# The down projection's weights: one transfer of 1.75 MiB in place of two halves

## The chip, the cores and the metric

The kernel runs on one core of a Trainium2 chip. The metric is the device time of one execution in microseconds. Three runs of the kernel before took 213.03, 213.16 and 212.81 us, a median of 213.03 us.

A core has five engines that run on their own and meet only through semaphores: TensorE (PE in the profile, with its weight loads listed as PEld), VectorE (DVE), ScalarE (ACT), GpSimd (POOL) and SyncE (SP). In this kernel SP issues nearly all the DMA transfers, one after the other in the order of its program.

## What is computed

The input is `x` of 2048 rows by 512 columns, in bf16. It is layer-normalised, and two blocks read the result. The output is the sum of three terms.

```python
xn = _layernorm(x)
# block A, linear attention with 32 heads of 16
qkv = xn @ wqkv                        # 512 -> 3 * 512, split into q, k, v
phi = lambda t: where(t > 0, t + 1, exp(t)) + 1e-6
kv  = einsum("bhsd,bhse->bhde", phi(k), v)
z   = einsum("bhsd->bhd", phi(k))
o   = (phi(q) @ kv) / (phi(q) . z + 1e-6)
A   = o @ wo                           # 512 -> 512
# block B, a gated feed-forward net with F = 1792
B   = (silu(xn @ w_gate) * (xn @ w_up)) @ w_down
out = x + A + B
```

The weights this document is about are those of the last product: `w_down`, 1792 rows by 512 columns in bf16, which is 1.75 MiB.

## The kernel before, in words

The 2048 rows are cut into 16 tiles of 128 rows, and four tiles make a chunk of 512 columns of the transposed input. F is cut into 14 blocks of 128.

First part. Each tile is loaded, normalised and transposed into `xnT`. TensorE projects it to k and q (L421), ScalarE, GpSimd and VectorE apply phi, and TensorE gathers the sum over rows of normalised input times phi(k) in four PSUM banks (L470). The order of all these steps is written out by hand, as a string of words that `run` reads (from L562 on). A letter names the step and a number the tile, so `Q11` is the q projection of tile 11. The letter `T` takes one of the big weight loads from the list `BIG` (L548). `T0` is the first half of the gate weights, `T5` and `T4` the second halves of the up and gate weights, and `T6` and `T7` the two halves of the down weights. `U0` and `U1`, near the end of the string, are the first two gate and up blocks.

Second part. A loop over 56 steps `j` (four chunks of 14 blocks) multiplies the gate and the up weights with `xnT` (`gu`, L524). ScalarE applies silu to the gate product (L532) and VectorE multiplies it with the up product into `hT` (L537). Between these steps lie the rest of the attention (the products at L582 and L648, the sum `z` turned by a DMA at L598 and spread over partitions by the transfers at L605 and L607, the division, and the transposes by DMA at L641). The output tiles come in the chunks after the first: `otile` runs when the block number is 5, 8, 11 or 13, and tiles 12 to 15 follow the loop, the last of them in three cuts. An output tile is one PSUM accumulation of 4 products with the attention part (L654) and 14 products with the down weights (L658). VectorE adds `x` (L664) and SP stores the tile (L667).

How order and waits come about. Every step calls `K.add` with an engine, its instructions, the keys it reads and the keys it writes. `number` works out from the keys which earlier operations each one waits for, and leaves out a wait that the engine is known to have passed. `emit` then writes each engine's program in the order of the calls. So the order of the words matters only among steps of one engine. A transfer has a semaphore of its own. Every load goes through the helper at L184 and is known in the profile by its tile.

The down weights are kept whole in `wd`, 14 blocks of 512 columns on each partition. `dload` (L205) loads seven blocks. Its two calls are the last two entries of `BIG`, both on SP and with nothing of SP's between them: the words between `T6` and `T7` give work to the other engines only. Both loads write a key of their own, nobody has read or written `wd` before, and so neither waits for anything. The only reader is the second half of `ogroup` at L658, which names both keys. The first output tile is therefore the first that waits for them.

Of the kernel before, what the change touches and what calls it, by code (L numbers as in the profile page):

```python
# [10 lines left out]
P = 128  # L11
# [7 lines left out]
NFC = F // P  # L19
# [92 lines left out]
def bass_parallel_sum__linear_attn_block__swiglu_ffn__prompt_kernel(nc, A_x, A_wqkv, A_wo, B_x, B_w_gate, B_w_up, B_w_down, out):  # L112
    xin = A_x[0]
    oview = out[0]
    K = _Program()
    bf, f32 = dt.bfloat16, dt.float32

    with contextlib.ExitStack() as es:
        E = es.enter_context

        def sb(name, shape, dtype):
            return E(nc.sbuf_tensor(name, shape, dtype))
# [15 lines left out]
        wd = sb("wd", [P, NFC, D], bf)  # L138
        pk = sb("pk", [P, NT, D], bf)
        pq = sb("pq", [P, NT, D], bf)  # L140
        hT = sb("hT", [P, 2, NFC, 512], bf)
# [37 lines left out]
        def B(i):  # L179
            return ("bank", i)  # L180


        def load(eng, key, dst, src):
            K.add(eng, lambda e: e.dma_start(dst, src), w=[key], dma=True)  # L184
# [14 lines left out]
        def fload(eng, key, dst, src, h):  # L199
            load(eng, (key, h), dst[:, :, h * FH:(h + 1) * FH],  # L200
                 src[:, h * FH:(h + 1) * FH].rearrange("(c p) f -> p c f", p=P))

        WD_LO = (0, 7)

        def dload(eng, lo):  # L205
            load(eng, ("wd", lo), wd[:, lo:lo + 7, :],
                 B_w_down[lo * P:(lo + 7) * P, :].rearrange("(c p) f -> p c f", p=P))


        K.add("act", lambda e: e.preload_act_table_set("natural_log_exp_and_others"))  # L210
# [332 lines left out]
        def pair(j):  # L543
# [4 lines left out]
        BIG = [lambda: fload("sp", "wg", wg, B_w_gate, 0), lambda: fload("sp", "wu", wu, B_w_up, 0),  # L548
               lambda: wload("sp", 2), lambda: woload("sp"),
               lambda: fload("sp", "wg", wg, B_w_gate, 1), lambda: fload("sp", "wu", wu, B_w_up, 1),  # L550
               lambda: dload("sp", WD_LO[0]), lambda: dload("sp", WD_LO[1])]
        steps.update({"U": pair, "T": lambda t: BIG[t]()})

        def run(text):
# [14 lines left out]
            T2 K14 u9 P0 s10 x14 K7 n10 S12 R11 u10 m14 x7 m7 T3 Q6 S8 y6 R12 G10 K6 s14 R8 P12 D12 n6 x6 Q7 s7  # L569
            S15 L8 R15 G7 m6 u6 y7 s6 Q14 y14 D8 G14 Q12 P11 K12 n7 u7 y12 Q8 L15 x12 n14 n12 D0 m12 u14 D11 K8  # L570
            u12 s12 y8 n8 G6 G12 x8 K11 u8 m8 D15 s8 Q11 x11 K15 T0 Q15 y11 G8 x15 m11 T5 s11 y15 n11 m15 G11 T4
            u11 T6 n15 s15 u15 U0 G15 U1 T7
        """)

        def gt_evac(c, eng):
# [76 lines left out]
        def ogroup(bank, t, lo, hi):  # L652
            C, jj = t // 4, t % 4
            fns = [(lambda e, g=g: e.matmul(  # L654
                banks[bank][:, 0:hi - lo], pk[:, t, g * P:(g + 1) * P], M[:, g, lo:hi],
                start=(g == 0), stop=False)) for g in range(NG)]
            K.add("pe", fns, r=[("pk", t)] + [("M", g) for g in range(NG)], w=[B(bank)])
            fns = [(lambda e, fc=fc: e.matmul(  # L658
                banks[bank][:, 0:hi - lo], hT[:, C % 2, fc, jj * P:(jj + 1) * P], wd[:, fc, lo:hi],
                start=False, stop=(fc == NFC - 1))) for fc in range(NFC)]  # L660
            K.add("pe", fns, r=[("hT", C % 2, fc) for fc in range(NFC)] + [("wd", lo_) for lo_ in WD_LO], w=[B(bank)])

        def oout(bank, t, lo, hi):
            K.add("dve", lambda e: e.tensor_tensor(  # L664
# [5 lines left out]
        def otile(t):  # L670
            b = t % 4
            ogroup(b, t, 0, D)
            oout(b, t, 0, D)
# [8 lines left out]
        for j in range(NGU):  # L682
            C, fc = j // NFC, j % NFC
# [33 lines left out]
        for b, lo, hi in cuts:  # L717
            ogroup(b, 15, lo, hi)
            oout(b, 15, lo, hi)
# [37 lines left out]
```

## Time and profile before

| | |
|---|---|
| median of three runs | 213.03 us (212.81 to 213.16) |
| the profiled execution | 213.13 us, of which the span of its instructions is 211.9 us |
| clock granted to TensorE | 1.00 |
| busy: PE, DVE, ACT, POOL | 207.1, 124.5, 68.4, 67.1 us |
| read from HBM, written to it | 9.96 MB, 2.10 MB |

The span runs from the first to the last instruction of the program. A view called the chain of waits goes back from the last instruction, at each step to what released it. A group is all instructions of one line, engine, operation and tile, with the mean duration of one. Matmuls are pipelined, so their durations overlap, and the distance from one start to the next is shorter than the duration of one. Idle time of an engine stands with what ended it. For a transfer the profile gives the time that its issue took on the queue of the issuing engine, and the time from issue to landing. "SPq" is SP's queue. A view in windows gives the busy time of each engine in a stretch, the clock granted to TensorE, the mean busy share of the 16 DMA engines and the rate at which they moved bytes.

### The profile page before, as it was taken

The numbers are of one execution on the slowest core, as the hardware profiler recorded it, in microseconds if no ns is written. First come the engines' busy times: TensorE is split into PE (matmuls) and PEld (weight loads), VectorE is DVE, ScalarE is ACT, GpSimd is POOL, SyncE is SP. The second block draws the span as 40 slices with busy tenths as digits, with TensorE's granted clock in tenths as the row PEclk, the third lists the DMA queues.
The fourth block names the chain that finished last, engine by engine and source line by source line (L and its number), as shares of the span: only waits on it lengthen the run. The fifth ranks groups of instructions, "written<-read, shape, count | busy, mean of one in ns | idle before, by whom it ended". The sixth has DMA issues, their size and how long they took to land.

```text
span 211.9 us, 2730 instructions
## 1 busy us (share of the span) xinstructions
PE 207.1 (98%) x994; PEld 97.1 (46%) x1013; DVE 124.5 (59%) x223; ACT 68.4 (32%) x146; POOL 67.1 (32%) x95
## 2 busy tenths in 40 slices
PE   7999999999999999999999999999999999999995
PEld 3534444444544444444444444444444444444455
DVE  3799998653996368454644773464457473535121
ACT  5994656554344333031221322130123031220000
POOL 3795688649950162202202121202202220000000
DMA  5963547599501201120101110111010111011001
GB/s 164 359 197 77 124 102 223 101 338 365 164 0 25 53 0 25 24 53 25 25 25 46 28 29 25 25 50 25 28 33 20 23 50 50 3 50 47 27 28 51
DMA packets 28750, 16.44 MB, mean 78 GB/s; under 512 B 18624, under 2 KB 28608, under 8 KB 28736
## 3 DMA queue, kind: packets, MB, share of 16 engines
q1 hardware_dynamic: 27872, 15.48, 26.3%
q10 hardware_dynamic: 864, 0.79, 1.1%
q8 instruction: 8, 0.13, 0.3%
q14 instruction: 6, 0.05, 0.1%
HBM read 9.96 MB, written 2.10 MB: 57 GB/s over the span
## 4 chain that ended last, share of the span: by engine, by line
PE 93%; ACT 3%; DMA 1%; issue 1%; DVE 1%; POOL 0%
PE pb L524 45%; PE pb L658 23%; PE pb L421 11%; PE pb L654 7%; PE pb L470 6%; ACT ef L439 1%; DMA x_sb<-in_A_x_dram 1%; PE pb L382 0%; PE pb L582 0%; PE pb L648 0%; DVE stats L254 0%; ACT rstd L263 0%; ACT lnv L261 0%; ACT xnT L356 0%; PE pb L244 0%
## 5 line engine op out<-in xcount | busy, mean ns | idle before, releaser
L532 ACT ACTIVATE sil<-pb 128x512 bf16<-128x512 f32 x56 | 33.4, 597 | 104.1 <-PE pb L524 102.5
L537 DVE TENSOR_TENSOR hT<-pb,sil 128x512 bf16<-128x512 f32 x56 | 38.2, 682 | 38.1 <-PE pb L524 37.5
L524 PE MATMUL pb<-xnT,wg 128*128 128x512 bf16 x224 | 57.8, 379 | 0.0
L524 PE MATMUL pb<-xnT,wu 128*128 128x512 bf16 x214 | 55.8, 379 | 0.5
L658 PE MATMUL pb<-wd,hT 128*128 128x512 bf16 (+2 forms) x247 | 51.1, 355 | 0.3
L615 POOL TENSOR_TENSOR pz<-pq,zbc 128x512 f32<-128x512 bf16 x16 | 22.3, 1395 | 91.4 <-DVE den L622 79.1
L658 PEld LDWEIGHTS pb<-wd,hT 128*128 128x128 bf16 x252 | 23.6, 98 | 24.9
L524 PEld LDWEIGHTS pb<-xnT,wu 128*128 128x128 bf16 x224 | 21.9, 98 | 26.0
L524 PEld LDWEIGHTS pb<-xnT,wg 128*128 128x128 bf16 x224 | 21.9, 98 | 25.9
L664 DVE TENSOR_TENSOR out_sb<-pb,x_sb 128x512 bf16<-128x512 f32 (+2 forms) x18 | 11.4, 632 | 35.8 <-PE pb L658 35.8
L421 PE MATMUL pb<-wqkv,xnT 128*128 128x512 bf16 x102 | 23.8, 379 | 0.5 <-ACT xnT L356 0.4
L442 ACT ACTIVATE ef<-pb 128x512 bf16<-128x512 f32 x26 | 15.3, 593 | 12.5 <-PE pb L421 12.5
L449 POOL TENSOR_SCALAR ef<-ef 128x512 bf16<-128x512 bf16 x26 | 15.9, 615 | 8.7 <-ACT ef L442 8.7
L654 PE MATMUL pb<-M,pk 128*128 128x512 bf16 (+2 forms) x72 | 16.8, 355 | 0.0
L421 PEld LDWEIGHTS pb<-wqkv,xnT 128*128 128x128 bf16 x104 | 10.1, 98 | 12.9 <-ACT xnT L356 0.9
L254 DVE BATCH_NORM_STATS2 stats<-x_sb 128x6 f32<-128x512 bf16 x16 | 10.8, 678 | 3.5 <-DMA x_sb<-in_A_x_dram 3.5
L470 PE MATMUL pb<-pk,xn 128*128 128x512 bf16 x51 | 12.8, 379 | 0.1
L637 DVE TENSOR_TENSOR pq<-pq,rden 128x512 bf16<-128x512 bf16 x16 | 12.6, 786 | 0.0
L622 DVE TENSOR_REDUCE den<-pz 128x32 f32<-128x512 f32 x16 | 10.8, 676 | 0.0
L493 POOL TENSOR_TENSOR zacc<-zacc,pk 128x512 f32<-128x512 f32 x8 | 10.2, 1278 | 0.6
L460 DVE SCALAR_TENSOR_TENSOR pk<-pb,ef 128x512 bf16<-128x512 f32 x13 | 8.7, 679 | 2.6 <-POOL ef L449 2.6
L460 DVE SCALAR_TENSOR_TENSOR pq<-pb,ef 128x512 bf16<-128x512 f32 x13 | 8.8, 682 | 2.5 <-POOL ef L449 2.4
(70 smaller groups left out, 112.6 us busy)
## 6 DMA issues: line engine op xcount, KB each, us to landing
x_sb<-in_A_x_dram SPq DMA_DIRECT2D x15, 128.0 KB, 4.6
out_dram<-out_sb SPq DMA_DIRECT2D x15, 128.0 KB, 1.7
wu<-in_B_w_up_dram SPq DMA_DIRECT2D x2, 896.0 KB, 7.1
wg<-in_B_w_gate_dram SPq DMA_DIRECT2D x2, 896.0 KB, 7.1
wd<-in_B_w_down_dram SPq DMA_DIRECT2D x2, 896.0 KB, 12.9
wqkv<-in_A_wqkv_dram ACTq DMA_DIRECT2D x5, 128.0 KB, 4.8
wqkv<-in_A_wqkv_dram SPq DMA_DIRECT2D x1, 512.0 KB, 4.1
wo<-in_A_wo_dram SPq DMA_DIRECT2D x1, 512.0 KB, 4.9
```

What stands on the lines that cost most here:

```text
L421: fns.append(lambda e, c=c, first=first, last=last: e.matmul(banks[b][:, :], src[:, c, t * P:(t + 1) * P], wqkv[:, c, col:col + D], start= ...
L442: K.add("act", lambda e: e.activation(buf, banks[b][:, :], ACT.Exp), r=[B(b)], w=[bkey])
L449: K.add("pool", lambda e: e.tensor_scalar(out=buf, in0=buf, scalar1=top, scalar2=0.0, op0=ALU.min, op1=ALU.max), r=[bkey] + tkeys, w=[bkey])
L460: K.add("dve", lambda e: e.scalar_tensor_tensor(out=dst, in0=val, scalar=low, in1=mid, op0=ALU.max, op1=ALU.add), r=keys + lkeys, w=[dkey])
L470: K.add("pe", [(lambda e, c=c: e.matmul(banks[c][:, :], src[:, t, c * P:(c + 1) * P], pk[:, t, :], start=first, stop=last)) for c in range ...
L524: fns.append(lambda e, c=c, b=b, w_=w_: e.matmul(banks[b][:, :], w_[:, c, fc * P:(fc + 1) * P], xnT[:, c, C * 512:(C + 1) * 512], start=(c ...
L532: K.add("act", lambda e: e.activation(sil[:, j % 2, :], banks[gb(j)][:, :], ACT.Silu), r=[B(gb(j))], w=[("sil", j % 2)])
L537: K.add("dve", lambda e: e.tensor_tensor(out=hT[:, C % 2, fc, :], in0=banks[gb(j) + 1][:, :], in1=sil[:, j % 2, :], op=ALU.mult), r=[B(gb( ...
L615: K.add("pool", lambda e: e.tensor_tensor(out=pz[:, t % 2, :].rearrange("q (g p) -> q g p", g=NG), in0=pq[:, t, :].rearrange("q (g p) -> q ...
L637: K.add("dve", lambda e: e.tensor_tensor(out=heads(pq[:, t, :]), in0=heads(pq[:, t, :]), in1=rden[:, i, :][:, :, None].broadcast_to([P, NH ...
L654: fns = [(lambda e, g=g: e.matmul(banks[bank][:, 0:hi - lo], pk[:, t, g * P:(g + 1) * P], M[:, g, lo:hi], start=(g == 0), stop=False)) for ...
L658: fns = [(lambda e, fc=fc: e.matmul(banks[bank][:, 0:hi - lo], hT[:, C % 2, fc, jj * P:(jj + 1) * P], wd[:, fc, lo:hi], start=False, stop= ...
```

## The change

The two loads of seven blocks become one load of fourteen. `BIG` loses an entry, the string loses its last word `T7`, and the reader at L658 names one key instead of two. The transfer's place in SP's order is that of `T6`.

```diff
-        WD_LO = (0, 7)
-
-        def dload(eng, lo):
-            load(eng, ("wd", lo), wd[:, lo:lo + 7, :],
-                 B_w_down[lo * P:(lo + 7) * P, :].rearrange("(c p) f -> p c f", p=P))
+        def dload(eng):
+            load(eng, ("wd",), wd[:, :, :], B_w_down.rearrange("(c p) f -> p c f", p=P))
...
-               lambda: dload("sp", WD_LO[0]), lambda: dload("sp", WD_LO[1])]
+               lambda: dload("sp")]
...
-            u11 T6 n15 s15 u15 U0 G15 U1 T7
+            u11 T6 n15 s15 u15 U0 G15 U1
...
-            K.add("pe", fns, r=[("hT", C % 2, fc) for fc in range(NFC)] + [("wd", lo_) for lo_ in WD_LO], w=[B(bank)])
+            K.add("pe", fns, r=[("hT", C % 2, fc) for fc in range(NFC)] + [("wd",)], w=[B(bank)])
```

## The prediction

> **What bounds the kernel now.** I read the page first, then the chain of waits in order of time, then what PE waited for, and last the down weights themselves: when they are issued, when they land, and when they are first used.
>
> The page, its head, its slices and its shares of the chain:
>
> ```profile
> span 211.9 us, 2730 instructions
> PE 207.1 (98%) x994; PEld 97.1 (46%) x1013; DVE 124.5 (59%) x223; ACT 68.4 (32%) x146; POOL 67.1 (32%) x95
> ...
> PE   7999999999999999999999999999999999999995
> ...
> DMA  5963547599501201120101110111010111011001
> ...
> PE 93%; ACT 3%; DMA 1%; issue 1%; DVE 1%; POOL 0%
> ```
>
> TensorE is busy in every slice but the first and the last, and 93% of the chain that ended last is its work. The DMA engines are full in slices 8 to 10 only; a slice is 211.9 / 40 = 5.3 us, so that is about 42 to 58 us. That is where the down weights travel.
>
> The chain of waits in order of time (start, duration, what), some of its pieces, and all that PE waited for over the whole span (total, times, longest):
>
> ```profile
> 0.81 2.65 DMA x_sb<-in_A_x_dram
> ...
> 12.52 1.90 PE pb L421 x8
> ...
> 46.36 1.73 PE pb L470 x8
> ...
> 165.53 3.02 PE pb L658 x14
> ...
> 209.69 0.29 DVE out_sb L664
> ```
>
> ```profile
> PE pb L244 <- PEq L742: 0.8, 1, 0.8
> PE pb L421 <- ACT xnT L356: 0.4, 1, 0.4
> PE pb L382 <- POOL nmb L368: 0.3, 1, 0.3
> ```
>
> PE waits three times, 1.5 us together. The last of the waits is the one that ends at 12.52 us, where the chain passes from ACT to PE for good. From there to the last product of the output the chain stays on PE, to 209.69 us, and the only other pieces are issue gaps of 0.05 us. So 197 of 211.9 us are one unbroken row of matmuls. A change helps only by having fewer of them, closer together, or by a shorter head (12.5 us) or tail (2.2 us). It hurts only by opening a hole in the row.
>
> **The change part by part.** First, when the weights come and when they are wanted. The instructions that touch the tile `wd` (duration in ns, min/median/max, first and last start in us; the time to landing below), then the same restricted to the first of the two loads:
>
> ```profile
> L658 PEld LDWEIGHTS pb<-wd,hT x252: 97/98/98, 85.7 to 209.4; 128*128 128x128 bf16 x126
> ...
> L184 SPq DMA_DIRECT2D wd<-in_B_w_down_dram x2: 793/1950/3108, 42.8 to 43.6; - x2
> ...
> DMA to landing us min/median/max: 12.1/12.9/13.7
> ```
>
> ```profile
> L184 SPq DMA_DIRECT2D wd<-in_B_w_down_dram x1: 793/793/793, 42.8 to 42.8; - x1
> ...
> DMA to landing us min/median/max: 12.1/12.1/12.1
> ```
>
> The first half is issued at 42.8 us and lands 12.1 us later, at 54.9. The second is issued at 43.6 and lands 13.7 us later, at 57.3. The first instruction that reads `wd` is a weight load at 85.7 us. The slack is 85.7 - 57.3 = 28.4 us.
>
> *The landing of the single transfer.* The bytes are the same, 2 x 896 KB, and they stand behind the same gate and up weights. The stretches around them (PE busy, PEld, DVE, ACT, POOL, clock, DMA share, GB/s):
>
> ```profile
> 46.00:48.00 2.00, 2.00 (x11) 0.94 (x10) 1.66 (x3) 1.72 (x3) 1.53 (x3) 1.00 1.05 392
> ...
> 54.00:55.00 1.00, 1.00 (x5) 0.46 (x5) 1.00 (x2) 0.00 (x0) 0.92 (x2) 1.00 1.10 348
> 55.00:56.00 1.00, 0.95 (x6) 0.48 (x6) 1.00 (x2) 0.60 (x1) 0.92 (x2) 1.00 0.44 138
> 56.00:57.00 1.00, 1.00 (x12) 0.65 (x11) 1.00 (x2) 0.00 (x0) 0.92 (x2) 1.00 0.06 20
> 57.00:58.00 1.00, 1.00 (x13) 0.65 (x11) 1.00 (x3) 0.60 (x1) 1.00 (x1) 1.00 0.00 0
> ```
>
> The engines are full up to 55 us and empty from 57. The pipe has no hole that merging could close, so the last byte cannot come much before 56. I take 57 us. The bounds: 55 us, where the full stretch ends, and 70.2 us, if the one transfer took as long as both in turn (42.8 + 2 x 13.7). Even the late end leaves 15.5 us before 85.7. Cost on the path: 0. If the cover were gone, each microsecond of landing after 85.7 would be a microsecond of the kernel.
>
> Here a rule can be held against the rows. The two halves land 57.3 - 54.9 = 2.4 us apart, and 917,504 bytes at 348 GB/s take 2.6 us, so the second pays nothing beside its bytes. The Trainium skill, "DMA: Bandwidth & Descriptors", section "Anatomy of one DMA", fits each transfer of another issuing path with about 2.0 us fixed plus its bytes. By that fixed cost, paid in turn, the merged transfer would land some 2 us sooner, an estimate from the page; the trace does not agree for transfers queued behind each other, and the sum is the same either way.
>
> *The halves' separate keys.* A half that lands early could let an early reader start. The only reader names both keys, and both are down 28.4 us before it. Cost 0.
>
> *SP's queue.* The issues in time (start, duration):
>
> ```profile
> 41.06 0.58 SPq L184 DMA_DIRECT2D wg<-in_B_w_gate_dram  x1
> ...
> 42.79 3.94 SPq L184 DMA_DIRECT2D wd<-in_B_w_down_dram  x2
> 64.21 1.20 SPq L598 DMA_TRANSPOSE zT<-zb  x1
> 67.67 0.34 SPq L605 DMA_DIRECT2D zrow<-zc  x1
> ```
>
> The two issues hold SP to 46.7 us, the second longer (3.1 us) than the first (0.8 us), as if it had to wait for room. One issue is removed. What the longer one costs the trace does not show: at least 0.34 us, as the shortest issue in these rows, at most twice 3.94 = 7.9 us. I take 3.9, since the same number of pieces must fit. SP is then free between 43.1 and 50.7 us. What is next on SP is the transpose of `z` at 64.21, which is not late for SP's sake: `z` is summed only in step 6 of the loop. At least 13.5 us of cover. Cost 0, gain 0. No transfer is moved past another: `T0`, `T5` and `T4` stay ahead.
>
> *The gate weights, which are tight.* The tile `wg` within 40 to 70 us:
>
> ```profile
> L524 PEld LDWEIGHTS pb<-xnT,wg x48: 97/98/98, 47.7 to 70.0; 128*128 128x128 bf16 x48
> ...
> L184 SPq DMA_DIRECT2D wg<-in_B_w_gate_dram x2: 507/544/580, 41.1 to 42.2; - x2
> ...
> DMA to landing us min/median/max: 5.3/7.1/8.9
> ```
>
> The first half of `wg` is issued at 41.06 and lands 5.3 us later, at 46.4; PE reads it at 47.7. The margin is only 1.3 us, the smallest that I found near the edit. But this load is issued 1.7 us before the down weights, in the same queue, so its bytes stand ahead of theirs before and after. Bounds: a gain of 0, since PE does not wait there, and a loss of 0 unless it landed 1.3 us later. I take 0.
>
> *TensorE's program.* The first L658 group loses one of its two waits for `wd`. There is no hole in PE's row there, so a wait passed long ago costs nothing that shows. Bounds: the 0.05 us of an issue gap, and 0. I take 0.
>
> *Contention between transfers and matmuls.* The 8 matmuls from 46.36 us, under 392 GB/s, take 1.73 us, 0.216 each; the 14 from 165.53, with little traffic, take 3.02, also 0.216. The full pipe does not slow PE now, and one transfer cannot fill it fuller. Cost 0.
>
> The sum: 213.13 us, the profiled execution's own time (span 211.9, the other 1.2 us around it), plus 0. It stands 0.1 us above the median of 213.03, so I predict 213.0 us.
>
> **The rivals.**
>
> *Slower: fewer DMA engines carry the merged transfer.* A transfer of another shape could be spread over fewer of the 16. The down bytes begin to flow when the second half of `wg` is down, at 42.2 + 8.9 = 51.1 us, and PE needs them at 85.7. 1,835,008 bytes in 34.6 us are 53 GB/s; an engine carries 348 / 16 = 21.75 GB/s, so it decides from two engines downward. With two: 42.2 us, landing at 93.3, 7.6 us of stall, 220.6 us. Against it: the halves, of the same layout, keep all 16 engines at a share of 1.10. The Trainium skill, "DMA: Bandwidth & Descriptors", section "Why a DMA increments its semaphore by 16 and not by 1", says that the slowest dimension of both patterns decides the number of engines. If that were the 14 blocks instead of the 128 partitions, 14 engines would carry it and nothing would be late; the trace's share speaks for 16. Chance 0.02.
>
> *Slower: TensorE's instructions come late.* They too come by DMA. The queues within 40 to 60 us (packets, MB, share):
>
> ```profile
> q1 hardware_dynamic: 4266, 4.79, 73.0%
> q8 instruction: 1, 0.02, 0.4%
> ```
>
> One block of instructions travels on q8 in the crowded stretch. If it waited behind a longer transfer until PE ran dry, PE would stop. The price lies between nothing and the time of a transfer in the queue there, 12.1 us; about 2 us is what I would expect of it, near a small load's 2.65 us in the chain above, so 215 us. Against it: PE has no such stop now with the same bytes queued, and its program is the same up to 85.7 us. Chance 0.09.
>
> *The head comes out otherwise.* PE's three waits in the first 12.5 us follow from the landing of `x` (2.65 us in the chain) and a row of small operations. The edit touches nothing there, but the program is a new build with one semaphore and one transfer less, and the three runs already differ by 0.35 us. If the first load landed 0.5 us sooner, 212.5 us; all three waits gone would be 211.5. As much later, 213.5. Chance 0.15 for faster by more than 0.2%, 0.11 for slower.
>
> *The change does what it says but nobody sees it.* This is the forecast: 28.4 us of slack hide it. Chance 0.63.
>
> **How the numbers follow.** 0.2% of 213.03 is 0.43 us, about what a measurement of this kernel can tell from no change. The forecast (0.63) lies within it. Slower: 0.02 + 0.09 + 0.11 = 0.22. Faster: 0.15. The range takes in the forecast and the head's half microsecond on both sides with a little over, 212.5 to 213.7. Left out are the two stalls (0.11) and the far ends of the head (some 0.06). The forecast's own range is 212.6 to 213.46.
>
> **What would show it.** In the profile after: one issue of `wd` of 1792 KB on SP at 42.8 us, lasting 3 to 5 us; landing near 57 us; full DMA engines to 55 and none after 58; the first weight load of L658 at 85.7; SP's next issue at 64.2; the three PE waits and no fourth. The prediction is wrong if PE shows a wait between 12.5 and 209.7 us, if `wg`'s first read is later than 47.7, or if the head does not end at 12.5.

## The result and the profile after

The changed kernel takes 212.56 us (median of 22 runs, 212.39 to 213.05), the kernel before 213.01 us (22 runs, 212.80 to 213.36). The ratio is 0.998, with a 95% interval of 0.9973 to 0.9986. That is 0.45 us less: a small gain, but a real one, and it lies just beyond the 0.43 us (0.2%) that the prediction called no change. The profiled execution took 212.57 us, its span 211.3 us.

The page after: head, PE's slices, the queues of instruction blocks (packets, MB, share), and the issue of the down weights (KB, us to landing).

```profile
span 211.3 us, 2728 instructions
PE 207.0 (98%) x994; PEld 97.0 (46%) x1013; DVE 124.5 (59%) x223; ACT 68.4 (32%) x146; POOL 67.2 (32%) x95
...
PE   7999999999999999999999999999999999999996
...
q8 instruction: 8, 0.13, 0.3%
q14 instruction: 5, 0.04, 0.1%
...
wd<-in_B_w_down_dram SPq DMA_DIRECT2D x1, 1792.0 KB, 14.6
```

PE has the same work, the same busy time to 0.1 us, and still three waits (total, times, longest), with lines three lower for the shorter source:

```profile
PE pb L241 <- PEq L739: 0.8, 1, 0.8
PE pb L418 <- ACT xnT L353: 0.4, 1, 0.4
PE pb L379 <- POOL nmb L365: 0.2, 1, 0.2
```

So the gain is not in the middle. Two instructions are gone: one issue on SP and one wait on TensorE. The chain of waits after, at the pieces shown of before:

```profile
0.81 2.56 DMA x_sb<-in_A_x_dram
...
12.36 1.90 PE pb L418 x8
...
46.20 1.73 PE pb L467 x8
...
165.37 3.02 PE pb L655 x14
...
209.53 0.29 DVE out_sb L661
```

Everything from 12.36 us on is the old row, 0.16 us earlier, to its end at 209.53 instead of 209.69. So 0.16 us of the profiled 0.56 come from the head, and 0.4 us must lie behind 209.53, in the tail. The last output transfer, in the view of the tile `out_sb` from 209.5 us on, first before, then after (duration of the issue in ns, start; time to landing):

```profile
L667 SPq DMA_DIRECT2D out_dram<-out_sb x1: 333/333/333, 210.0 to 210.0; - x1
...
DMA to landing us min/median/max: 1.8/1.8/1.8
```

```profile
L664 SPq DMA_DIRECT2D out_dram<-out_sb x1: 332/332/332, 209.8 to 209.8; - x1
...
DMA to landing us min/median/max: 1.4/1.4/1.4
```

The same 32 KB land in 1.4 us instead of 1.8. In exact times, before: issued at 210.011, landed at 211.847, 1.84 us. After: 209.849 and 211.294, 1.45 us. That is the other 0.39 us.

The trace says more. A transfer lands in sixteen shares, each with an event of its own. Before, fifteen shares are down by 211.542 and the last comes 0.31 us later. After, all sixteen come between 211.125 and 211.294. And in the kernel before, a block of instructions is fetched while that transfer travels; in the changed kernel this comes later. The queues within 210.6 to 211.0 us, before:

```profile
q1 hardware_dynamic: 103, 0.02, 27.4%
q14 instruction: 1, 0.01, 4.8%
```

The same stretch in the changed kernel, and then its stretch from 211.4 to 212 us:

```profile
q1 hardware_dynamic: 144, 0.03, 37.5%
```

```profile
q14 instruction: 1, 0.01, 4.0%
```

Before, one packet of 8192 bytes on q14 starts at 210.685 us and takes 0.307 us, while the last output is on its way. After, the corresponding packet starts at 211.465, when the output is down. SP's last act is two waits for its last outputs. They end with the span. So I took the block to be fetched at a fixed place of SP's program, and the removed issue to have moved the rest of the program by one instruction against that place: "the end theory".

### The profile page after: what moved, and what is told of

Its sections match the earlier page's. It is cut to its first block, busy times and chain, and to the rows that moved or that the text cites. A ratio compares the mean times of both kernels' runs of the same rounds, so it can differ in the third digit from the quotient of the medians.

```text
span 211.3 us, 2728 instructions
## 1 busy us (share of the span) xinstructions
PE 207.0 (98%) x994; PEld 97.0 (46%) x1013; DVE 124.5 (59%) x223; ACT 68.4 (32%) x146; POOL 67.2 (32%) x95
## 4 chain that ended last, share of the span: by engine, by line
PE 94%; ACT 3%; DMA 1%; issue 1%; DVE 1%; POOL 0%
PE pb L521 46%; PE pb L655 23%; PE pb L418 11%; PE pb L651 7%; PE pb L467 7%; ACT ef L436 1%; DMA x_sb<-in_A_x_dram 1%; PE pb L579 0%; PE pb L379 0%; PE pb L645 0%; DVE stats L251 0%; ACT rstd L260 0%; ACT lnv L258 0%; ACT xnT L353 0%; PE pb L241 0%
## 5 line engine op out<-in xcount | busy, mean ns | idle before, releaser
L439 ACT ACTIVATE ef<-pb 128x512 bf16<-128x512 f32 x26 | 15.3, 593 | 12.5 <-PE pb L418 12.5
## 6 DMA issues: line engine op xcount, KB each, us to landing
wd<-in_B_w_down_dram SPq DMA_DIRECT2D x1, 1792.0 KB, 14.6
```

The source lines that it names most:

```text
L439: K.add("act", lambda e: e.activation(buf, banks[b][:, :], ACT.Exp), r=[B(b)], w=[bkey])
```

## The experiments

Each kernel was timed in five rounds against the kernel before on the same chip. I count SP's program in instructions of the built program: 84 before, 83 after (the trace records two fewer of each kernel). The waits that some kernels add are satisfied when SP reaches them, 39 us earlier; they do nothing but take up a place.

**The changed kernel again.** No edit.

> The changed kernel once more, as the base of this comparison. What I think now (the end theory): the last output transfer lands 1.84 us after its issue before (210.011 to 211.847 us) and 1.45 us after (209.849 to 211.294), because before a block of 8192 bytes of instructions is fetched at 210.685 us on one of the DMA engines that carry this transfer, and after it is fetched at 211.465, when the transfer is down. The block's fetch would follow from the length of SP's program, which lost one instruction. The rival (the weights theory): the single transfer itself makes the gain. Both expect 212.5 to 212.6 us here against 213.0 for the kernel before, ratio 0.998. The end theory expects the fetch again behind the last landing, and a last landing of about 1.45 us. A third theory (the head) gives the gain to the first loads of x: 2.65 us in the chain before, 2.56 after; it expects that the end of the head keeps to within 0.05 us of the changed kernel's first profile.

Measured: 212.68 us, ratio 0.9982 (0.9973 to 0.9990). The last landing took 1.44 us, the block came at 211.619, behind it. The head ended at 12.42 us, 0.07 later than in the first profile, outside the 0.05 that the head theory asked for.

**The changed kernel with a useless wait on SP (84 instructions).**

```diff
+        def idle_waits(eng, n):
+            K.add(eng, [lambda e: e.wait_ge(sems["dma", 0], 16) for _ in range(n)], r=[("x", 0)])
...
-               lambda: dload("sp")]
+               lambda: (idle_waits("sp", 2), dload("sp"))]
```

(Two waits, since one is folded into the transfer's own instruction. The lines of the views are those of each kernel's own source.)

> The changed kernel, with one more instruction on SP's queue: a wait for the first tile of x, satisfied 39 us earlier, just ahead of the single transfer of the down weights. SP's program is as long as before the change (84 instructions instead of 83), TensorE's stays one shorter. End theory: the block is fetched near 210.7 us again, the last landing takes 1.8 us, and the time is 212.9 to 213.1 us, ratio 0.9995 to 1.0005. Weights theory, and a theory that gives the gain to TensorE's shorter program: 212.5 to 212.6 us, ratio 0.998.

Measured: 213.14 us, ratio 1.0004 (0.9996 to 1.0013). The gain is gone with the single transfer in place. The view of `out_sb` from 209.5 us on:

```profile
L667 SPq DMA_DIRECT2D out_dram<-out_sb x1: 333/333/333, 209.7 to 209.7; - x1
...
DMA to landing us min/median/max: 2.1/2.1/2.1
```

The block started at 210.620 us, 0.94 us after the last issue. Fifteen shares landed 1.54 us after it, the sixteenth 0.56 us later. The head of this execution ended at 12.19 us, earlier than in either profile of the changed kernel, and the kernel is still slower. So neither the weights nor the head make the difference, nor does TensorE's program, which is one shorter here too.

**Two halves, the second issued on ScalarE's queue (SP 83).**

```diff
-               lambda: dload("sp", WD_LO[0]), lambda: dload("sp", WD_LO[1])]
+               lambda: dload("sp", WD_LO[0]), lambda: dload("act", WD_LO[1])]
```

> The kernel before, two halves, with the second half issued on ScalarE's queue instead of SP's, at its place in the written order. SP's program has 83 instructions as after the change, TensorE's has its two waits as before, ScalarE's has one instruction more. The half is issued some 10 us later and must be down before 85.7 us, which leaves over 15 us. End theory: the block comes after the last landing, 212.5 to 212.65 us, ratio 0.998. Weights theory and the theory of TensorE's program: 213.0 us, ratio 1.000.

Measured: 212.53 us, ratio 0.9978 (0.9965 to 0.9991). The last landing took 1.44 us. The whole gain is there without the merged transfer, and with TensorE's program at its old length.

**The changed kernel with one more instruction still (SP 85).** As with 84, with four waits; two of them share an instruction in the trace and one is folded into the transfer's.

> The changed kernel with two more instructions on SP's queue than it has, 85 in all, both waits that are long satisfied. End theory: the fetch moves one instruction earlier than before the change, to the issue of the last output transfer, near 210.5 us. Its 0.31 us then end by 210.8, just ahead of the bytes of that transfer (211.0 to 211.1 us before). If that is enough to be out of the way, 212.55 us; if the fetch still delays one engine's share, 213.0. Weights theory: 212.5 to 212.6 us.

Measured: 212.56 us, ratio 0.9983 (0.9973 to 0.9992). The fetch started earlier than I had expected: at 209.273, 0.42 us ahead of the last issue at 209.697. The last landing took 1.44 us. The block was not out of everybody's way: it met the output before, issued at 208.692, whose sixteenth share came 0.43 us late. But that output was down at 210.667, ahead of the last one, and cost nothing. A place too many is as good as a place too few.

**Three and four transfers instead of one (SP 85 and 86).**

```diff
+        WD_CUTS = ((0, 5), (5, 10), (10, 14))
+
         def dload(eng):
-            load(eng, ("wd",), wd[:, :, :], B_w_down.rearrange("(c p) f -> p c f", p=P))
+            for lo, hi in WD_CUTS:
+                load(eng, ("wd", lo), wd[:, lo:hi, :],
+                     B_w_down[lo * P:hi * P, :].rearrange("(c p) f -> p c f", p=P))
```

For four transfers the cuts are `((0, 4), (4, 7), (7, 11), (11, 14))`; the reader at the products names all of them.

> The down weights in three transfers (blocks 0 to 4, 5 to 9, 10 to 13) on SP's queue, one more than before the change instead of one fewer. SP's program has 85 instructions, TensorE's is as long as before. End theory: the block of instructions is fetched ahead of the last output's issue (0.4 us ahead of it, as in the merged kernel with 85), the last landing takes 1.44 us, and the time is 212.55 us, ratio 0.998: cutting the load finer gains as much as merging it. Weights theory: 213.0 us or more, since the number of transfers went the other way.

> The same in four transfers, 86 instructions on SP. End theory: the fetch moves one more step ahead, to about 208.3 us, where it can meet only the landing of an earlier output; last landing 1.44 us, 212.55 us, ratio 0.998. Weights theory: 213.0 us or more.

Measured: 212.49 us, ratio 0.9979 (0.9970 to 0.9988), and 212.47 us, ratio 0.9976 (0.9966 to 0.9986). The issues and landings of the four transfers:

```profile
L184 SPq DMA_DIRECT2D wd<-in_B_w_down_dram x4: 761/1050/2962, 42.5 to 45.5; - x4
...
DMA to landing us min/median/max: 11.0/11.4/11.6
```

Cutting the load finer gains as much as merging it. What gains is to leave the length of 84.

**A place fewer than the change (SP 82).** The attention's output weights go out on ScalarE's queue.

```diff
-               lambda: wload("sp", 2), lambda: woload("sp"),
+               lambda: wload("sp", 2), lambda: woload("act"),
```

> The changed kernel with the attention's output weights (wo, 512 KB) issued from ScalarE's queue at their place in the written order, so that SP's program has 82 instructions. End theory: the fetch stays behind the last landing, or does not come in the program's time at all; last landing 1.44 us, 212.55 us, nothing gained beyond 83. A theory in which each instruction on SP costs something would give another 0.4 us, 212.1.

Measured: 212.56 us, ratio 0.9976 (0.9968 to 0.9985), landing 1.44 us, the block at 211.606, behind the end. Nothing beyond what 83 gives, so an instruction on SP has no price as such.

**The kernel before, again.**

> The kernel before once more, for a second look at its tail. All theories: 213.0 us, ratio 1.000. End theory: the block fetched 0.6 to 0.95 us after the last output's issue, and the last landing 1.8 to 2.1 us after it.

Measured: 213.06 us, ratio 0.9999 (0.9990 to 1.0008). The block started at 210.356, 0.68 us after the last issue, and the landing took 1.84 us: fifteen shares in 1.51 us, the sixteenth 0.33 later. The head ended at 12.18 us, the earliest of all these profiles:

```profile
12.18 1.90 PE pb L421 x8
```

So the 0.16 us that the first pair of profiles showed in the head are what one execution differs from another.

**The kernel before with a useless wait (SP 85).** The edit of the wait again, ahead of the first half; both halves stay.

> The kernel before, its two halves untouched, with one useless instruction more on SP ahead of the first half: a wait that is long satisfied. SP's program has 85 instructions. End theory: the block is fetched 0.4 us ahead of the last output's issue, the last landing takes 1.44 us instead of 1.84, and the time is 212.55 us, ratio 0.998, though only work was added. Weights theory: 213.0 us, ratio 1.000.

Measured: 212.66 us against 213.24 for the kernel before on this chip, ratio 0.9969 (0.9956 to 0.9983). Only work was added. The queues within 209.2 to 209.9 us with the output before the last one (KB, us to landing), then the same output in the kernel before, and the tile `out_sb` from 209.5 on, with the useless wait again:

```profile
q1 hardware_dynamic: 83, 0.02, 12.7%
q14 instruction: 1, 0.01, 5.4%
...
out_dram<-out_sb SPq DMA_DIRECT2D x1, 32.0 KB, 2.0
```

```profile
out_dram<-out_sb SPq DMA_DIRECT2D x1, 32.0 KB, 1.4
```

```profile
L670 SPq DMA_DIRECT2D out_dram<-out_sb x1: 332/332/332, 210.0 to 210.0; - x1
...
DMA to landing us min/median/max: 1.4/1.4/1.4
```

All kernels in one table. "Fetch" is the start of the last block on q14 against the issue of the last output; "late share" is how far the sixteenth share of that output came behind the fifteenth.

| kernel | SP's program | fetch, us | last landing, us | late share, us | ratio to before |
|---|---|---|---|---|---|
| one transfer, `wo` on ScalarE's queue | 82 | +1.86 | 1.44 | 0.01 | 0.9976 |
| one transfer (the change) | 83 | +1.62, again +1.70 | 1.45, again 1.44 | 0.01, again 0.01 | 0.9980, again 0.9982 |
| two halves, one on ScalarE's queue | 83 | +1.67 | 1.44 | 0.02 | 0.9978 |
| two halves (before) | 84 | +0.67, again +0.68 | 1.84, again 1.84 | 0.31, again 0.33 | 0.9999 |
| one transfer, useless wait | 84 | +0.94 | 2.10 | 0.56 | 1.0004 |
| one transfer, useless waits | 85 | -0.42 | 1.44 | 0.02 | 0.9983 |
| two halves, useless wait | 85 | -0.44 | 1.43 | 0.02 | 0.9969 |
| three transfers | 85 | -0.45 | 1.45 | 0.03 | 0.9979 |
| four transfers | 86 | -2.15 | 1.44 | 0.03 | 0.9976 |

The kernels fall in two groups, by the length of SP's program and by nothing else that was varied: with 84 instructions the block is fetched while the last output travels, one share of it comes 0.3 to 0.6 us late, and the time is that of before. None of the others differs clearly from the change: the medians lie between 212.47 and 212.68 us, and their intervals overlap.

The fetch does keep to a place of SP's program. In all eleven profiles it starts 1.1 to 1.6 us after the end of the same instruction, the 79th that the trace records of SP, though against the last issue it moves by 4 us.

The packets of the trace show how block and output meet. With 84 instructions the block meets the last output. With 85 it starts 0.55 to 0.58 us after the issue of the output before, and meets that one. With 86 it falls between two outputs, and with 82 and 83 behind them all. Each share ends with a closing packet of 4 bytes. In each of the six meetings the last closing packet of the output starts 0.11 us after the block's end. In the kernel with one transfer and 84 instructions it is plainest: fifteen shares have started their closing packets by 210.768 us, the block ends at 210.927, and the eight data packets of the sixteenth share start from 210.923 on. So that share stands behind the block. In all six the late share then lands 0.69 to 0.75 us after its closing packet, the other fifteen 0.42 to 0.49 us after theirs, and the shares of the last two outputs, where no block meets them, 0.33 to 0.39 us. In the kernel before, this slower landing is nearly all of the lateness: the last two closing packets start 3 ns apart, the last two landings lie 0.31 us apart.

With 85 instructions the output that is met lands 1.88 to 2.00 us after its issue, against 1.44 to 1.46 for the same output elsewhere, and is down between 210.67 and 210.94 us. The last output follows between 211.13 and 211.38 and alone sets the end. Here a late share cost time only where no other output came after it.

## Why the prediction was right and wrong

The measured 212.56 us lies in the range, and the forecast of nothing on the path of the weights was right. But no change was forecast, and there is one: the ratio's interval excludes 1, and the time lies 0.04 us below the forecast's own range of 212.6 to 213.46. The case that came true, by that little, is the one that I gave 0.15, and not for the reason I gave it. That the whole range holds the result is luck: I had widened it for the head, and the gain is in the tail.

*Landing and slack* held. The single transfer was issued at 42.6 us and landed 14.6 us later, at 57.2; the forecast was 57. After, the stretches (PE, PEld, DVE, ACT, POOL, clock, DMA share, GB/s) and the first reader:

```profile
54.00:55.00 1.00, 0.95 (x5) 0.49 (x5) 1.00 (x2) 0.13 (x1) 0.99 (x1) 1.00 1.09 344
55.00:56.00 1.00, 1.00 (x7) 0.50 (x6) 1.00 (x2) 0.47 (x1) 0.92 (x2) 1.00 0.25 80
56.00:57.00 1.00, 1.00 (x11) 0.63 (x9) 1.00 (x2) 0.00 (x0) 0.92 (x2) 1.00 0.05 18
57.00:58.00 1.00, 1.00 (x11) 0.63 (x9) 1.00 (x3) 0.60 (x1) 1.00 (x1) 1.00 0.00 0
```

```profile
L655 PEld LDWEIGHTS pb<-wd,hT x252: 97/98/98, 85.6 to 209.2; 128*128 128x128 bf16 x126
```

The pipe is full to 55 us and all but empty from 56, and 28.4 us of slack remain. *Separate keys*, *gate weights*, *TensorE's program* and *contention* held: the kernel with two halves and 83 instructions has both waits and the whole gain, the first half of `wg` lands at 40.9 + 5.2 = 46.1 and is read at 47.6, and 8 matmuls under 391 GB/s still take 1.73 us.

*SP's queue* is the step that failed, twice. Its size was off without consequence: I took 3.9 us for the issue of the single transfer.

```profile
L184 SPq DMA_DIRECT2D wd<-in_B_w_down_dram x1: 792/792/792, 42.6 to 42.6; - x1
```

It took 0.79 us. The 3.1 us of the second half were not for the bytes, then: the same bytes in two transfers hold SP 3.94 us, in four 5.95. What SP waits for in that time is not shown. And "Cost 0, gain 0" for the removed issue was wrong. I asked what the instruction's time was worth and what was queued behind it, and not where the rest of SP's program moves to. It moved by one place, the block's fetch by 0.94 us against the last issue, and the tail gave back 0.4 us.

*The rivals.* "Fewer DMA engines" did not happen. "TensorE's instructions come late" had the right kind of traffic, and the wrong engine, place and sign: I looked at q8 between 40 and 60 us, where the weights are, and not at q14 in the last 2 us, where a late byte is a late end. Nothing runs dry; a fetch gets in the way of an output. "The head comes out otherwise" had the right sign for the wrong place: across these kernels the head's end moves between 12.18 and 12.52 us, and the kernel before has both ends of that. So my sign that the prediction is wrong if the head does not end at 12.5 us came true (12.36) and meant nothing. I named the tail's 2.2 us as a place where a change can help and then priced only the head. One reading of the page was loose, without consequence: the DMA engines are nearly full in the second slice too, and half full in slice 10.

The Trainium skill, "Runtime: NRT & Kernel Launch", section "Instruction fetch mechanics", says that each sequencer fetches its program in blocks over a DMA queue of its own, and that a block boundary is mostly hidden. The trace agrees that the blocks travel by DMA, and TensorE stops for none: it waits three times, all in the head. Here one block of SP's is not hidden, since it costs 0.4 us when it meets the last output. The page gives 16 KiB for a block; these are 8192 bytes on q14 and 16,384 on q8.

## What to carry to other kernels

When the middle of a kernel is one unbroken row on one engine, small differences come from its two ends, so look at the landing of the last transfer, share by share, before crediting an edit far away. Adding or removing an instruction shifts the rest of that engine's program against its blocks; a difference of some tenths of a percent can be tested by adding a useless instruction to the faster kernel or to the slower one. Here that test moved the whole gain both ways, so the merged transfer itself is worth nothing that these runs can tell, and the next edit on SP can lose it again.

## What the runs showed of the hardware that I had not expected

- A block of 8192 bytes of instructions, one packet of 0.307 us when it met the last output, goes with a last landing that is 0.4 to 0.65 us longer: 1.84, 1.84 and 2.10 us, against 1.43 to 1.45 in the eight profiles where it did not meet it. The trace does not name the DMA engines. That the block and the late share use the same one is inferred from the last closing packet, 0.11 us after the block's end in all six meetings. Why that share then lands 0.69 to 0.75 us after its closing packet, and why the other fifteen are slower by some 0.1 us too (down 1.51 to 1.54 us after the issue instead of 1.41 to 1.44, for the last output), is open.
- The block is fetched 1.1 to 1.6 us after the same instruction of SP in all eleven profiles. One instruction more or less in front of it decides which output it meets, if any.
- SP itself stands 0.44 to 0.46 us behind that instruction in the four profiles with 82 or 83 instructions, with nothing recorded that it waits for, and its last wait still ends with the last landing, so it costs nothing here. In the others the next instruction is an output's issue, which has to wait for its data anyway.
- The issue of 1792 KB holds SP no longer (0.79 us) than the issue of the first 896 KB did (0.79 us); the second half's took 3.1 us. From the start of the first issue to the end of the last, the same bytes take 0.79, 3.94, 4.61 and 5.95 us in one, two, three and four transfers.
